# Attention and MLP in one kernel: zeros for 22 early matmuls written first, weight decoding begun later, one sink product for two heads

## The chip, the cores and the metric

The kernel runs on one core of a Trainium2 chip. The time is the device time of one execution in microseconds, the median of three runs. The engines are TensorE (PE, with its weight loads PEld), VectorE (DVE), ScalarE (ACT), GpSimd (POOL) and SyncE (SP), which issues most DMAs.

## The reference

Attention over 4 batches and 8 heads (768 positions, head size 64) with a window of 128 and 4 sink positions, then an MLP on the 3072 tokens:

```python
scores = scale * np.matmul(q, k.transpose(0, 1, 3, 2))
keep = (pos[None, :] < n_sink) | ((rel >= 0) & (rel < window))      # 4, 128
scores = np.where(keep, scores, -1000000000.0)
a = np.exp(scores - max); a = a / (sum + 1e-09)
x = np.matmul(a, v)                       # then heads side by side: 3072 x 512
h = x @ w_in                              # 512 x 2048
g = np.maximum(0.01 * h, h)
return (g @ w_out).astype(np.float32)     # 2048 x 512
```

The MLP's weights arrive as 64-bit floats.

## The kernel before, in words

The queries are cut into 8 units (`NU`): a batch and one half of its positions, 384 queries (`TU`). Units 0 and 1 (`EARLY = 2`) take a short way through attention in plain 32-bit floats; the later ones split their numbers into a high and a low part. Within a unit the 8 heads come one by one, and two heads make a pair (`NPAIR` = 4), which gives one 128-row slice of the MLP's input.

A head has three blocks of queries, j = 0 to 2. For each, `scores` (L264) multiplies queries and keys on PE, `softmax_early` takes the masked maximum on VectorE (L276, `pe`) and the exponential on ScalarE (L278). `normalise_early` (L281 to L288) divides by the sums; `tail_early` transposes on PE (L336, L337, L340) and copies to `pt` on ScalarE (L338, L341). The four sink positions go by their own way: `sk` on GpSimd (L344), one transpose for both heads (L370), and `sn` on VectorE (L374), whose rows hold head and position, with zeros where a row does not belong to a query block. `values` (L406) multiplies with the values of each head, the window blocks first, then the sinks: the left operand is that head's 64 columns of `sv` (from the load `vsraw`), the right one is `sn`, and the product goes into that head's 64 rows of the pair's accumulator `acc` (tile `v`). The rows of `vsraw` are zero in the columns of the other head. After the second head, `emit_x` makes the two parts `xh` (ScalarE, L474) and `xl` (VectorE, L475).

The MLP has 16 steps for each unit: `h` (L519), `g` (L526, L527), its parts `gh` and `gl`, and the sum over steps `o` (L540). A weight pair for one step (`wi`, `wo`) is loaded as raw 64-bit words (`wiraw`, `woraw`, 512 KB each) and decoded by `load_weights`: three operations on VectorE for each of the two (L170, L172, L174, tiles `di`/`do` and `wif`/`wof`), a copy on ScalarE (L178) and a subtraction on GpSimd (L179). In unit 0's MLP step fc the pairs up to fc + 2 are decoded (`AHEAD`). A load beyond the first four waits for the fourth decoding before it (`DEPTH`).

PE's instructions stand in the order in which the code writes them (`MANUAL`): first a loop over the steps of attention until unit 0 is through and a little of unit 1, then MLP steps with attention steps between. The other engines' order, and that of the DMAs, is made by a scheduler. In the first loop `PRE`, `PRE0` and `PRED` say how many weight pairs are decoded there, from which step, and how many steps apart. `WARM` matmuls of zeros (`wz`, L564, tile `warm`), whose product nobody reads, are written before everything else on PE in the code.

```python
        if done >= PRE0 and len(wts) < 2 * min(PRE, (done - PRE0 + 1) // PRED):
            load_weights(len(wts) // 2)
```

`check_weights` later loads raw weights once more (`ciraw`) and looks at their range; it is off the way of the results.

Of the kernel before, what the change touches and what calls it, by code (L numbers as in the profile page):

```python
# [20 lines left out]
P = 128  # L21
# [9 lines left out]
TU = T * P  # L31
# [19 lines left out]
XLP = 3  # L51
VSW = 1
AHEAD = 2
PRE = 3
WARM = 16
DEPTH = 4
PRE0 = 4
PRED = 6
W_LO = 1.125 * 2.0 ** -15
W_HI = 1.875 * 2.0 ** 16  # L60
KSL = ((0, P), (0, W3), (WM, W3)), ((0, W3), (WM, W3), (2 * WM, W3))
# [47 lines left out]


@with_exitstack
def fast_path(ctx, tc, cpool, qk, vu, vs, w_in, w_out, out, ident, lim, masks, tri, diag, negm, wmin, wmax):
    nc = tc.nc
    wpool = ctx.enter_context(tc.tile_pool(name="wpool", bufs=1))
    apool = ctx.enter_context(tc.tile_pool(name="apool", bufs=2))
# [6 lines left out]
    ps_t = ctx.enter_context(tc.tile_pool(name="ps_t", bufs=1, space=PSUM))  # L122
    ps_v = ctx.enter_context(tc.tile_pool(name="ps_v", bufs=1, space=PSUM))

    wz = wpool.tile([P, TU], mybir.dt.bfloat16, name="wz")
    nc.vector.memset(wz, 0.0)
    zeros = iopool.tile([SKR, TU], F32, tag="io", name="zeros")
    nc.vector.memset(zeros, 0.0)
    sts = []
    for half in range(2):  # L130
        st = wpool.tile([SKR, (T - 1 + half) * P], F32R, name=f"st{half}")
# [26 lines left out]
    def load_weights(fc):  # L158
        for nm in ("i", "o"):
            raw = wpool.tile([P, 512, 2], I32, tag=f"w{nm}{fc}", name=f"w{nm}raw{fc}")  # L160
            dma = fetch(raw, nm, fc)
            if len(decoded) >= DEPTH:
                tc.add_manual_dep(dma.ins, decoded[-DEPTH].ins.name,
                                  mybir.DependencyInfo(mybir.DependencyClass.Sync, mybir.DependencyReason.SCHED_ONLY),
                                  reason="pace")
            top, low = raw[:, :, 1], raw[:, :, 0]
            word = ps_t.tile([P, 512], I32, tag="d", name=f"d{nm}{fc}")
            w = iopool.tile([P, 512], F32, tag="io", name=f"w{nm}f{fc}")
            with tc.issue_after(anchor[0].ins):
                nc.vector.tensor_scalar(out=word, in0=top, scalar1=3, scalar2=0x3FFFFFFF,  # L170
                                        op0=ALU.logical_shift_left, op1=ALU.bitwise_and)
            nc.vector.scalar_tensor_tensor(out=word, in0=top, scalar=-0x40000000, in1=word,  # L172
                                           op0=ALU.bitwise_and, op1=ALU.bitwise_or)
            decoded.append(nc.vector.scalar_tensor_tensor(out=w.bitcast(I32), in0=low, scalar=29, in1=word,  # L174
                                                          op0=ALU.logical_shift_right, op1=ALU.bitwise_or))
            both = wpool.tile([P, 2, 512], F32R, tag=f"w{nm}{fc}", name=f"w{nm}{fc}")
            hi, lo = both[:, 0, :], both[:, 1, :]
            nc.scalar.copy(out=hi, in_=w)  # L178
            nc.gpsimd.tensor_tensor(out=lo, in0=w, in1=hi.bitcast(F32), op=ALU.subtract)  # L179
            wts[nm, fc] = (hi, lo)  # L180
# [130 lines left out]
    def segments(half):  # L311
        if half:
            return (0, 0, P), (P, 0, 2 * P), (3 * P, P, 2 * P), (5 * P, 2 * P, P)
        return (0, 0, 2 * P), (2 * P, P, 2 * P), (4 * P, 2 * P, P)
# [70 lines left out]
    def values(u, h, pt, st, state):  # L385
        half = u % 2
        pair, odd = divmod(h, 2)
        q0 = 0 if half else P
        hp = slice(odd * D, (odd + 1) * D)
        lp = slice((1 - odd) * D, (2 - odd) * D)  # L390
        vv, sv = state["v"]
        if u < EARLY:
            if not odd:
                state["acc"] = ps_v.tile([P, 512], F32, tag="v", name=f"v{u}_{h}")
            out = state["acc"][hp, :]
            mms = [(vv[:, kb * P + odd * D:kb * P + (odd + 1) * D], pt[:, 0, po:po + m], qo, m)
                   for kb, (po, qo, m) in enumerate(segments(half))]
            mms.append((sv[0:st.shape[0], hp], st, q0, TU - q0))
        else:
            out = ps_v.tile([P, 512], F32, tag="v", name=f"v{u}_{h}")  # L400
            cs = slice(odd * P, (odd + 1) * P)
            mms = [(vv[:, kb, cs], pt[:, c, po:po + m], qo, m)
                   for kb, (po, qo, m) in enumerate(segments(half)) for c in range(2)]
            mms.append((sv[:, 0, cs], st, q0, TU - q0))
        for c, (l, r, o, m) in enumerate(mms):
            nc.tensor.matmul(out[:, o:o + m], lhsT=l, rhs=r, start=c == 0, stop=c == len(mms) - 1,  # L406
                             skip_group_check=True)
        if u < EARLY:
            x = state["acc"][:, 0:TU]
        else:  # L410
            if not odd:
                state["xf"] = xpool.tile([P, TU], F32, tag="xf", name=f"xf{u}_{pair}")
            x = state["xf"]
            nc.scalar.copy(out=x[hp, :], in_=out[lp, 0:TU])
            nc.vector.tensor_tensor(out=x[hp, :], in0=out[hp, 0:TU], in1=x[hp, :], op=ALU.add)  # L415
        if odd:
            emit_x(u, pair, x)
# [42 lines left out]
    def attend(u, h, pend, state):  # L460
        yield from (attend_early if u < EARLY else attend_late)(u, h, pend, state)
        if h % 2:
            state = state[h // 2 % 2]

            def gather():
                state["st"] = sinks(u, h // 2, state["sk"])
            pend.append((0, gather))
            for o in range(2):
                pend.append((1, lambda o=o: values(u, h - 1 + o, state["pt", o], state["st"], state)))

    def emit_x(u, pair, x):
        xh = xpool.tile([P, TU], F32R, tag=f"xh{pair}", name=f"xh{u}_{pair}")
        xl = xpool.tile([P, TU], F32R, tag=f"xl{pair}", name=f"xl{u}_{pair}")
        nc.scalar.copy(out=xh, in_=x)  # L474
        (nc.gpsimd if EARLY <= u < XLP else nc.vector).tensor_tensor(out=xl, in0=x, in1=xh.bitcast(F32), op=ALU.subtract)  # L475
        xs[u].append((xh, xl))
# [85 lines left out]
    flags = []  # L562
    for _ in range(WARM):
        nc.tensor.matmul(warm[:, 0:TU], lhsT=wz[:, 0:P], rhs=wz, start=True, stop=True)  # L564
# [3 lines left out]
    while done < att_steps + LEAD0:  # L568
        done += 1
        next(stream)  # L570
        if done >= PRE0 and len(wts) < 2 * min(PRE, (done - PRE0 + 1) // PRED):
            load_weights(len(wts) // 2)
# [148 lines left out]
def body(tc, qk0, qk1, vu0, vu1, vs, qT, kT, v, lims, w_in, w_out, out):  # L721
    nc = tc.nc
    w_in = w_in.bitcast(I32)
    w_out = w_out.bitcast(I32)
    with tc.tile_pool(name="cpool", bufs=1) as cpool:
        ident = cpool.tile([P, P], F32, name="ident")
        make_identity(nc, ident)
        negm = cpool.tile([P, 2 * B * H * T], F32, name="negm")
        wmin = cpool.tile([P, 2 * NFC], F32, name="wmin")
        wmax = cpool.tile([P, 2 * NFC], F32, name="wmax")  # L730
        with tc.tile_pool(name="tpool", bufs=1) as tpool:
            lim, masks, tri, diag = build_masks(nc, cpool, tpool, lims)
        flag = fast_path(tc, cpool, (qk0, qk1), (vu0, vu1), vs, w_in, w_out, out, ident, lim, masks, tri, diag,
                  negm, wmin, wmax)
        bad = nc.values_load(flag[0:1, 0:1], min_val=0, max_val=1)
        with tc.If(bad > 0):
            general_path(tc, qT, kT, v, w_in, w_out, out, ident, lim)
# [42 lines left out]
```

## Time and profile before

| what | value |
|---|---|
| median of 3 runs | 749.14 us (748.79 to 749.92) |
| the profiled execution | 746.63 us |
| its span on the core | 745.1 us |
| PE busy | 714.3 us, 96% of the span |
| VectorE, ScalarE, GpSimd busy | 74%, 56%, 50% of the span |
| mean granted clock of PE | 0.992 |
| DMA moved | 77.77 MB, 104 GB/s in the mean |

The profile gives each engine's busy time, the clock granted to PE (1 is full speed), and for idle time what ended it. Rows of the timeline read: start in us, duration in us, engine, line, operation, output from input, how many; in brackets the idle time ahead of it and what ended it. A row may stand for several instructions that follow each other; its duration goes from the first's start to the last's end. Durations of matmuls overlap, since PE pipelines them: what one costs in a full stream is the distance from its start to the next start.

### The profile page before, as it was taken

What the parts mean: (1) busy time and instruction counts of PE and PEld (TensorE: products, weight loads), DVE (VectorE), ACT (ScalarE), POOL (GpSimd) and SP (SyncE); (2) the same over time, 40 slices, a digit from 0 to 9 for tenths busy, and PEclk for the clock granted to TensorE, in tenths of its full rate; (3) what the DMA queues carried; (4) which work ended last, traced back from release to release, by engine and by line L of the source; (5) the groups of instructions that cost most, each with busy time, mean ns of one, the idle gap of its engine ahead of it and who ended that gap; (6) DMA issues with size and microseconds to landing.
All of it is one profiled execution on the core that took longest, in us unless ns stands there. A gap on an engine that the chain in (4) does not pass through costs nothing.

```text
span 745.1 us, 12489 instructions
## 1 busy us (share of the span) xinstructions
PE 714.3 (96%) x3881; PEld 620.6 (83%) x3881; DVE 549.3 (74%) x1749; ACT 420.6 (56%) x1178; POOL 370.0 (50%) x500
## 2 busy tenths in 40 slices
PE   4788999899999999999999999999999999999996
PEld 3446777679999988999988888999889899989995
DVE  6856798847667888888888888889888978733222
ACT  3556567656665666666666666666666655522221
POOL 2303446745445677665666587665666555300000
PEclk9899999999999999999999999999999999999999
DMA  8744675413212343225333443334332321001001
GB/s 295 228 132 127 195 219 172 146 36 99 58 51 65 119 125 114 92 94 156 115 106 102 132 130 100 104 98 153 109 109 78 112 68 40 0 1 43 1 1 48
DMA packets 43755, 77.77 MB, mean 104 GB/s; under 512 B 3616, under 2 KB 26400, under 8 KB 43680
## 3 DMA queue, kind: packets, MB, share of 16 engines
q1 hardware_dynamic: 41520, 74.66, 32.1%
q10 hardware_dynamic: 2160, 2.23, 1.2%
q8 instruction: 33, 0.54, 0.3%
q14 instruction: 42, 0.34, 0.2%
HBM read 70.58 MB, written 6.29 MB: 103 GB/s over the span
## 4 chain that ended last, share of the span: by engine, by line
PE 84%; DVE 9%; ACT 3%; issue 1%; DMA 1%; ACTq 0%; SPq 0%; DVEq 0%
PE o L540 32%; PE h L519 31%; PE v L406 10%; PE s L264 7%; PE t L349 2%; DVE gl L529 2%; DVE zeroi L192 1%; PE t L336 1%; DMA qkn<-in_qk 1%; DVE g L527 1%; DVE pe L276 0%; DVE xf L415 0%; DVE pk L309 0%; PE t L370 0%; PE t L337 0%
## 5 line engine op out<-in xcount | busy, mean ns | idle before, releaser
L519 PE MATMUL h<-xh,wi 128*128 128x384 f32 x1024 | 314.9, 354 | 1.6 <-DVE g L527 1.6
L540 PE MATMUL o<-wo,gh 128*128 128x512 f32 x768 | 244.4, 399 | 0.0
L519 PEld LDWEIGHTS h<-xh,wi 128*128 128x128 f32 x1024 | 190.0, 188 | 16.6 <-issue 2.9
L519 PE MATMUL h<-xl,wi 128*128 128x384 f32 x512 | 172.5, 337 | 0.0
L540 PE MATMUL o<-wo,gl 128*128 128x512 f32 x384 | 151.5, 394 | 0.0
L540 PEld LDWEIGHTS o<-wo,gh 128*128 128x128 f32 x768 | 133.7, 188 | 18.2 <-issue 2.4
L318 POOL TENSOR_SCALAR_AFFINE_SELECT pt<-stg 128x256 fp32r<-128x256 f32 x240 | 101.3, 447 | 83.4 <-DVE stg L357 70.1
L527 DVE TENSOR_TENSOR g<-h,g 128x384 f32<-128x384 f32 x128 | 71.0, 555 | 62.2 <-ACT g L526 60.4
L529 DVE TENSOR_TENSOR gl<-g,gh 128x384 fp32r<-128x384 f32 x112 | 93.3, 833 | 16.5 <-ACT gh L528 15.0
L526 ACT ACTIVATE g<-h 128x384 f32<-128x384 f32 x128 | 62.2, 486 | 71.5 <-PE h L519 71.1
L519 PEld LDWEIGHTS h<-xl,wi 128*128 128x128 f32 x512 | 96.9, 189 | 3.6 <-DVE xl L475 0.2
L230 POOL TENSOR_TENSOR qksp<-qkraw,qksp 64x392 fp32r<-64x392 f32 (+1 forms) x48 | 58.4, 1218 | 64.2 <-issue 47.5
L540 PEld LDWEIGHTS o<-wo,gl 128*128 128x128 f32 x384 | 72.2, 188 | 16.7 <-DVE gl L529 0.3
L303 ACT ACTIVATE pk<-pk,negm 128x128 f32<-128x128 f32 (+1 forms) x144 | 58.1, 403 | 48.6 <-DVE negm L300 47.8
L528 ACT CAST gh<-g 128x384 fp32r<-128x384 f32 x128 | 65.7, 513 | 33.7 <-DVE g L527 31.3
L264 PEld LDWEIGHTS s<-qksp 128*128 128x128 f32 x288 | 53.3, 188 | 5.9
L264 PE MATMUL s<-qksp 128*128 128x260 f32 (+1 forms) x288 | 56.2, 277 | 0.0
L232 POOL TENSOR_TENSOR qksp<-qkraw,qksp 128x384 fp32r<-128x384 f32 x48 | 53.5, 1115 | 3.6
L356 ACT CAST stg<-t 128x128 fp32r<-128x128 f32 x120 | 30.8, 256 | 42.6 <-PE t L349 32.2
L406 PEld LDWEIGHTS v<-pt,vsp 128*128 128x128 f32 x336 | 45.1, 189 | 5.8 <-issue 3.3
L229 ACT CAST qksp<-qkraw 128x776 fp32r<-128x776 f32 (+1 forms) x48 | 42.8, 892 | 11.3 <-PE s L264 11.0
L309 DVE TENSOR_SCALAR pk<-pk,sm 128x132 f32<-128x132 f32 (+1 forms) x120 | 46.0, 383 | 2.4
(131 smaller groups left out, 1088.0 us busy)
## 6 DMA issues: line engine op xcount, KB each, us to landing
qkraw<-in_qk SPq DMA_DIRECT2D x27, 454.0 KB, 3.3
qkraw<-in_qk SPq DMA_DIRECT2D x26, 388.0 KB, 3.1
wiraw<-in_w_in SPq DMA_DIRECT2D x16, 512.0 KB, 3.9
woraw<-in_w_out SPq DMA_DIRECT2D x16, 512.0 KB, 4.0
ciraw<-in_w_in SPq DMA_DIRECT2D x16, 512.0 KB, 3.8
coraw<-in_w_out SPq DMA_DIRECT2D x16, 512.0 KB, 3.6
out<-ob SPq DMA_DIRECT2D x23, 256.0 KB, 2.0
vraw<-in_vu SPq DMA_DIRECT2D x12, 256.0 KB, 2.7
```

The source lines that it names most:

```text
L230: nc.gpsimd.tensor_tensor(out=sp[D:P, TU:TU + n], in0=raw[D:P, TU:TU + n], in1=sp[D:P, TU:TU + n].bitcast(F32), op=ALU.subtract)
L232: nc.gpsimd.tensor_tensor(out=sp[:, TU + n:2 * TU + n], in0=raw[:, 0:TU], in1=sp[:, 0:TU].bitcast(F32), op=ALU.subtract)
L264: nc.tensor.matmul(ps[:, 0:kn], lhsT=sp[:, off + j * P:off + (j + 1) * P], rhs=sp[:, TU + k0:TU + k0 + kn], start=c == 0, stop=c == len(pa ...
L303: nc.scalar.activation(out=w, in_=w, func=AF.Exp, scale=-1.0, bias=neg, accum_out=sm)
L318: nc.gpsimd.affine_select(out=out, in_=src, pattern=([[0, x]] if x > 1 else []) + [[sign, P]], base=-1 if prev else 0, channel_multiplier= ...
L406: nc.tensor.matmul(out[:, o:o + m], lhsT=l, rhs=r, start=c == 0, stop=c == len(mms) - 1, skip_group_check=True)
L519: nc.tensor.matmul(ph[:, 0:TU], lhsT=w[:, cs], rhs=x, start=cc == 0 and c == 0, stop=cc == NCC - 1 and c == 2)
L526: nc.scalar.mul(g, ph[:, 0:TU], 0.01)
L527: anchor[0] = nc.vector.tensor_tensor(out=g, in0=ph[:, 0:TU], in1=g, op=ALU.max)
L528: nc.scalar.copy(out=gh, in_=g)
L529: (nc.gpsimd if u == 0 else nc.vector).tensor_tensor(out=gl, in0=g, in1=gh.bitcast(F32), op=ALU.subtract)
L540: nc.tensor.matmul(po[t], lhsT=gg[:, tsl], rhs=w, start=f == 0 and c == 0, stop=f == NFC - 1 and c == 2)
```

## The change

Four edits. The zeros `wz` are written as VectorE's first instruction, in `body`, and their number of matmuls goes from 16 to 22. Two weight pairs (before: three) are decoded in the first loop, from step 24 on and 12 steps apart (before: step 4 and 6 apart). In units 0 and 1 the sinks of a pair are one product with all 128 columns of `sv` into all 128 rows of `acc`, after the second head's window blocks; before, each head had its own.

```diff
-PRE = 3
-WARM = 16
+PRE = 2
+WARM = 22
 DEPTH = 4
-PRE0 = 4
-PRED = 6
+PRE0 = 24
+PRED = 12
...
-    wz = wpool.tile([P, TU], mybir.dt.bfloat16, name="wz")
-    nc.vector.memset(wz, 0.0)
...
-            mms.append((sv[0:st.shape[0], hp], st, q0, TU - q0))
...
         if u < EARLY:
+            if odd:
+                nc.tensor.matmul(state["acc"][:, q0:TU], lhsT=sv[0:st.shape[0], :], rhs=st, start=False, stop=True,
+                                 skip_group_check=True)
             x = state["acc"][:, 0:TU]
...
     with tc.tile_pool(name="cpool", bufs=1) as cpool:
+        wz = cpool.tile([P, TU], mybir.dt.bfloat16, name="wz")
+        nc.vector.memset(wz, 0.0)
```

What that does to the order of instructions, at three places. In the names, `s_1_0` is the score block 0 of head 1, `qkn_3` or `qkraw_2` the queries and keys of head 3 or 2, `pe_5` the weights of head 5; a number at the end only tells buffers apart. In the changed kernel lines between 126 and 395 are two lower than before.

PE, the start of the program, before (the warm matmuls' rows are cut to the first):

```order
L776 UNCONDITIONAL_BRANCH
L264 MATMUL s_0_0_196<-qkn_0_178 128x128
L264 MATMUL s_0_1_200<-qkn_0_178 128x260
L264 MATMUL s_0_2_204<-qkn_0_178 128x260
L564 LDWEIGHTS wz
L564 MATMUL warm<-wz 128x384
...
L264 MATMUL s_1_0_218<-qkn_1_184 128x128
```

And after:

```order
L778 UNCONDITIONAL_BRANCH
L564 LDWEIGHTS wz
L564 MATMUL warm<-wz 128x384
...
L262 MATMUL s_0_0_202<-qkn_0_184 128x128
L262 MATMUL s_0_1_206<-qkn_0_184 128x260
L262 MATMUL s_0_2_210<-qkn_0_184 128x260
L262 MATMUL s_1_0_224<-qkn_1_190 128x128
```

The warm matmuls moved from between head 0's and head 1's scores to the front of all.

SP, the loads after those of the first three heads, before:

```order
L202 DMA qkraw_2_187<-in_qk 128x776
L153 DMA wiraw_247<-in_w_in 128x4x256
L154 DMA woraw_257<-in_w_out 128x1024
L153 DMA wiraw_306<-in_w_in 128x4x256
L154 DMA woraw_316<-in_w_out 128x1024
L153 DMA ciraw_3055<-in_w_in 128x4x256
L202 DMA qkn_3_213<-in_qk 128x776
L202 DMA qkn_4_268<-in_qk 128x776
L153 DMA wiraw_359<-in_w_in 128x4x256
L202 DMA qkraw_5_330<-in_qk 128x776
```

And after:

```order
L200 DMA qkraw_2_193<-in_qk 128x776
L151 DMA ciraw_3053<-in_w_in 128x4x256
L151 DMA wiraw_410<-in_w_in 128x4x256
L152 DMA woraw_420<-in_w_out 128x1024
L151 DMA wiraw_503<-in_w_in 128x4x256
L152 DMA woraw_513<-in_w_out 128x1024
L200 DMA qkn_3_219<-in_qk 128x776
L200 DMA qkn_4_254<-in_qk 128x776
L200 DMA qkraw_5_296<-in_qk 128x776
L200 DMA qkn_6_343<-in_qk 128x776
```

Head 3's load stays behind the same five weight loads, of which the check copy is now the first; the third pair's load left its place among the heads' loads.

VectorE, heads 1 and 2, before (the read-outs `negm` behind each L276 are left out here and below):

```order
L170 TENSOR_SCALAR di_249<-wiraw_247 128x512
L276 ISA pe_2_274,negm<-s_2_0_277,m_84 128x128
...
L276 ISA pe_2_274,negm<-s_2_1_281,wide_143 128x260
...
L172 SCALAR_TENSOR_TENSOR di_249<-wiraw_247,di_249 128x512
L281 TENSOR_SCALAR sm_1_216<-sm_1_216 128x3
L174 SCALAR_TENSOR_TENSOR wif_250<-wiraw_247,di_249 128x512
L282 RECIPROCAL sm_1_216<-sm_1_216 128x3
L170 TENSOR_SCALAR do_259<-woraw_257 128x512
L288 TENSOR_SCALAR pe_1_215<-pe_1_215,sm_1_216 128x128
```

After, the first decoding stands between heads 5 and 6:

```order
L274 ISA pe_5_387,negm<-s_5_1_398,wide_143 128x260
...
L168 TENSOR_SCALAR di_412<-wiraw_410 128x512
L274 ISA pe_5_387,negm<-s_5_2_433,wide_151 128x260
...
L170 SCALAR_TENSOR_TENSOR di_412<-wiraw_410,di_412 128x512
L475 TENSOR_TENSOR xl_1_407<-v_2_394,xh_1_406 128x384
L172 SCALAR_TENSOR_TENSOR wif_413<-wiraw_410,di_412 128x512
L274 ISA pe_6_458,negm<-s_6_0_461,m_86 128x128
...
L168 TENSOR_SCALAR do_422<-woraw_420 128x512
```

The decoding moved from heads 1 to 4 to heads 5 to 7; its last operation of the two pairs stands just ahead of `xl_2`, and the third pair's six stand around `xl_3` and the MLP's first `g`.

More of the change, by code (lines that the diff above doesn't have):

```diff
@@ L111, in fast_path @@
 @with_exitstack
-def fast_path(ctx, tc, cpool, qk, vu, vs, w_in, w_out, out, ident, lim, masks, tri, diag, negm, wmin, wmax):
+def fast_path(ctx, tc, cpool, qk, vu, vs, w_in, w_out, out, ident, wz, lim, masks, tri, diag, negm, wmin, wmax):
     nc = tc.nc
@@ L732, in body @@
             lim, masks, tri, diag = build_masks(nc, cpool, tpool, lims)
-        flag = fast_path(tc, cpool, (qk0, qk1), (vu0, vu1), vs, w_in, w_out, out, ident, lim, masks, tri, diag,
+        flag = fast_path(tc, cpool, (qk0, qk1), (vu0, vu1), vs, w_in, w_out, out, ident, wz, lim, masks, tri, diag,
                   negm, wmin, wmax)
```

## Prediction

> **What bounds the kernel now.** I read the page first (busy shares, slices), then stages by window, then the timeline of the first 70 us, the DMA landings and the PE's waits.
>
> ```profile
> span 745.1 us, 12489 instructions
> PE 714.3 (96%) x3881; PEld 620.6 (83%) x3881; DVE 549.3 (74%) x1749; ACT 420.6 (56%) x1178; POOL 370.0 (50%) x500
> PE   4788999899999999999999999999999999999996
> PEclk9899999999999999999999999999999999999999
> 0.00:20.00 20.00, 10.00 (x45) 6.92 (x46) 14.16 (x57) 7.57 (x24) 5.50 (x19) 0.89 0.82 283
> 20.00:40.00 20.00, 16.16 (x66) 9.23 (x64) 15.76 (x48) 9.21 (x30) 6.95 (x8) 0.85 0.67 207
> 40.00:60.00 20.00, 17.23 (x83) 10.18 (x82) 10.11 (x45) 11.96 (x44) 0.76 (x4) 1.00 0.44 127
> 150.00:200.00 50.00, 50.00 (x276) 43.19 (x275) 29.54 (x107) 29.70 (x87) 24.14 (x34) 1.00 0.21 62
> ```
>
> The columns of a window are its length, then busy us (and instructions) of PE, PEld, DVE, ACT, POOL, the granted clock, the DMA share and GB/s. From 60 us on TensorE (PE) is full: 50.00 of 50.00 us in the last window. Of the 30.8 us in which it idles (745.1 less 714.3), 16.6 lie before 60 us (60 less 10.00, 16.16 and 17.23), and in the first two windows its clock is also below 1. PE runs its instructions in the written order, so the change can gain in two ways: PE reaches the first product of the MLP (58.74 us) sooner, or has less to do after it.
>
> **The change part by part. Warm-up and the first heads.**
>
> ```profile
> 0.94 0.38 DVE L104 MEMSET diag<- 24x384 f32 x1 [0.94 <-PEq L770]
> 6.12 2.53 PE L264 MATMUL s<-qkn 128*128 128x128 f32 x6 [6.12 <-DMA qkn<-in_qk]
> 8.00 0.28 DVE L276 CUSTOM_DVE_ANT_0 pe<-s,m 128x128 f32<-128x128 f32 x1
> 8.44 3.02 PE L564 MATMUL warm<-wz 128*128 128x384 bf16 x16
> 8.72 0.49 ACT L278 ACTIVATE pe<-pe,negm 128x260 f32<-128x260 f32 x1
> 10.31 0.82 DVE L288 TENSOR_SCALAR pe<-pe,sm 128x128 f32<-128x128 f32 x3
> 11.30 0.82 PE L264 MATMUL s<-qkn 128*128 128x128 f32 x4
> 9.58 3.67 SPq L202 DMA_DIRECT2D qkn<-in_qk  x2
> qkn<-in_qk SPq DMA_DIRECT2D x1, 388.0 KB, 8.2
> 20.14 0.63 PE L264 MATMUL s<-qkn 128*128 128x128 f32 x2
> 8.00:9.00 1.00, 1.00 (x4) 0.45 (x3) 0.84 (x6) 0.68 (x3) 0.75 (x5) 1.00 0.82 170
> 9.00:10.00 1.00, 1.00 (x8) 0.59 (x7) 0.33 (x3) 0.87 (x4) 0.00 (x0) 1.00 1.10 387
> ```
>
> Now the 16 warm matmuls stand behind head 0's scores and hold head 1's from 8.44 to 11.30: 2.86 us. With the zeros written at about 1.1 us (VectorE's first instruction starts at 0.94), the 22 can start at about 1.3. At the pace of these 16 (0.179 us) they take 3.9 us and end at 5.2, before head 0's data land at 6.12; at half that pace they end at 9.2. Either way VectorE's first softmax is held by the masks until about 8, so head 0 moves by -0.2 to +1.6 us and head 1's scores come 1 to 3 us sooner. The six more warm matmuls cost nothing: that wait for data covers them; without the cover they are 1.1 us.
>
> That is not passed on whole. On SP's queue head 3's load stands behind five weight loads of 512 KB, before and after. Before, it was issued at 9.58 and took 8.2 us: landed at 17.8. After, one of the five (the check copy) is put first and can go out at about 5 us, which fills the dip of 8 to 9 us (170 GB/s, beside 387 in the next microsecond): 217 GB/s for 1 us are 0.22 MB, 0.6 us at 387. Bounds: 0 (the dip stays) to 1 us (all of it). I take 0.5: landing at 17.3. PE is there earlier: head 0 is normalised near 11.1 as before (10.31 + 0.82); head 1's third scores and softmax wait for its transposes and end near 12.1; the exponential and its sum (0.49 + 0.2), the sums' reciprocal (0.35), the normalisation (0.82) and the sink copy and transposes (0.6) make about 14.6. So head 3's scores start at 17.3 instead of 20.14, and 2.7 us of wait on DMA is new. It also absorbs the worst case of the warm-up above.
>
> ```profile
> 15.00:16.00 1.00, 0.00 (x0) 0.00 (x0) 1.00 (x5) 0.31 (x3) 0.00 (x0) 0.89 1.11 425
> 16.00:17.00 1.00, 0.09 (x1) 0.12 (x1) 1.00 (x3) 0.50 (x1) 0.42 (x1) 0.50 1.03 406
> 22.00:23.00 1.00, 1.00 (x5) 0.59 (x4) 1.00 (x3) 0.33 (x1) 0.00 (x0) 0.70 0.96 328
> 20.70 2.21 PE L406 MATMUL v<-pt,vraw 128*64 128x256 f32 x6
> 43.98 1.30 PE L406 MATMUL v<-pt,vraw 128*64 128x256 f32 x6
> 25.85 0.33 PE L340 MATMUL t<-ident,pe 128*128 128x128 f32 x1
> 39.20 0.33 PE L340 MATMUL t<-ident,pe 128*128 128x128 f32 x1
> 48.21 0.33 PE L340 MATMUL t<-ident,pe 128*128 128x128 f32 x1
> 22.85 0.64 PE L406 MATMUL v<-sn,vsraw 16*64 16x256 f32 x2
> 23.42 0.71 PE L264 MATMUL s<-qkn 128*128 128x260 f32 x2
> ```
>
> The clock: PE idle from 13.85 brought the grant to 0.50 near 15.9, and it came back near 22.7, 4.5 us after PE had work again. Six value products take 2.21 us in it and 1.30 at full clock. After the change PE is sparse from 8.7 to 17.3 (some 2.7 us of work), so I expect half clock at 17.3, back within 2.4 to 5.8 us. Head 3's first scores, a set of value products, the second scores, another set and one sink product are 0.3 + 1.2 + 0.6 + 1.2 + 0.6 = 4.0 us at full clock (row starts). At 1.30/2.21 = 0.59 of it for 4.1 us, the middle, 2.4 are done, and 1.6 are left: 5.7 (5.0 to 6.4 at the ends). So head 2's first transpose (25.85 before) comes at 23.0: 2.85 us sooner; at full clock it would be 4.5.
>
> The Trainium skill, TensorE: Matmul & The Clock Gate, section "Part 1: The HAM clock gate", says that warmth is about 3.4 us of sustained activity, however many matmuls, and that an idle window of that length throttles again. By that rule the 22 early matmuls buy nothing at 17 us, as the term of 2.85 has it; if warmth lasted, the term would be 4.5. [...]
>
> **Heads 2 and 3 lose their decoding.** From head 2's first transpose to head 4's took 13.35 us (25.85 to 39.20) with decoding between, and the same stretch one pair later 9.01 without (39.20 to 48.21). After the change the earlier one is like the later one, less one sink product, 0.57 (22.85 to 23.42): 8.44. Lead at head 4's transpose: 2.85 + 13.35 - 8.44 = 7.8 (7 to 9.5).
>
> **Heads 4 to 7 gain it.**
>
> ```profile
> 13.28 0.69 DVE L170 TENSOR_SCALAR di<-wiraw 128x512 int32<-128x512 int32 x1
> 40.00 0.43 DVE L276 CUSTOM_DVE_ANT_0 pe<-s,wide 128x260 f32<-128x260 f32 x1 [2.06 <-PE s L264]
> 40.20:49.20 9.00, 7.97 (x39) 4.71 (x39) 5.26 (x25) 4.94 (x20) 0.38 (x2) 1.00 0.47 128
> 16.48 1.81 DVE L288 TENSOR_SCALAR pe<-pe,sm 128x128 f32<-128x128 f32 x3
> 16.58 1.30 POOL L179 TENSOR_TENSOR wi<-wif,wi 128x512 fp32r<-128x512 f32 x1 [5.20 <-ACT wi L178]
> ```
>
> Two pairs are 12 VectorE operations of 0.69: 8.3 us, and by the order all stand between head 5's second softmax and pair 2's split (`xl_2`). Cover: one fits the 2.06 us of idle before 40.00 (0.69), and VectorE idles 3.74 of the 9.00 us behind it (9.00 less 5.26). Left are 8.3 - 4.4 = 3.9; the bounds are 0 (all absorbed, were the idle longer) and 8.3 (none). Overlapped issue saves about 0.08 each, so I take 3.6. GpSimd's subtraction beside a normalisation stretches that from 0.82 to 1.81 us; one half overlap of the four: 0.4. While VectorE does this, PE waits; like the idle from 13.85 that can cost the clock, and I take an even chance of one more cold spell, 4.1 x 0.41 = 1.65: 0.8. What waits behind each decode operation is the next softmax, then the transposes, then PE. Against it pair 3's sink product goes, 0.57; that of pair 2 lies in PE's wait and is counted at nothing. Lead at the first MLP product (58.74): 7.8 - 3.6 - 0.4 - 0.8 + 0.6 = 3.6 (1 to 7).
>
> **Third pair and the second unit's sinks.**
>
> ```profile
> 60.23 0.56 DVE L475 TENSOR_TENSOR xl<-v,xh 128x384 fp32r<-128x384 f32 x1 [2.74 <-ACT xh L474]
> 62.89 0.55 DVE L527 TENSOR_TENSOR g<-h,g 128x384 f32<-128x384 f32 x1
> 63.49 0.44 PE L519 MATMUL h<-xh,wi 128*128 128x384 f32 x1 [1.59 <-DVE g L527]
> 80.02 0.85 PE L406 MATMUL v<-sn,vsraw 24*64 24x384 f32 x2
> 80.80 0.74 PE L540 MATMUL o<-wo,gh 128*128 128x512 f32 x2
> ```
>
> The third pair's six operations, 4.1 us, now come with the MLP's start. Two fit the 2.74 us of idle before `xl_3`, the rest pushes the second normalisation back by about 0.8 us, hardly the first `g`. I put 0.5 us of new PE wait (bounds -0.3, since one operation leaves the place ahead of `g`, and 2.7, the four that are not covered). In the second unit PE is full, so each removed sink product counts whole: 0.78 (80.02 to 80.80), four of them 3.1.
>
> Sum: 3.6 + 3.1 - 0.5 = 6.2 us. The profiled execution took 746.63 us (span 745.1), the median of the runs is 749.14, 2.5 more; the saving is the same against either: 740.4 in such a profile, 742.9 in the median.
>
> **Rivals.**
> - The clock stays full at 17 us and in the later gaps. For it: some work falls in every few us. Against: 0.50 after a like gap. Gain 6.2 + 1.65 + 0.8 = 8.7: 740.4.
> - Slower: VectorE sets the pace from head 4 into the MLP. If none of the moved decoding is covered (8.3, and 4.1 for the third pair) and every overlap with GpSimd costs 1 us (four: 4.0), the 7.8 + 0.6 + 3.1 = 11.5 turn into 4.9 us lost: 754.0. It decides from 11.5 exposed us on. For it: 13.35 against 9.01 us. Against: VectorE idles 3.74 of 9.00 us there.
> - The DMA order hurts: the check copy, put first, delays heads 1 and 2 by its transfer (512 KB, about 1.35 us at 388 GB/s), the dip is not filled (0.5), and the third pair stalls PE by 2.7 (2.2 more). Gain 6.2 - 4.0 = 2.2: 746.9.
> - The merged sink does not do what it says: with twice the columns of weights it costs twice, and 0.57 + 3.1 in the sum (and 0.57 each in pairs 0 and 1) goes. Gain 6.2 - 4.8 = 1.4: 747.7. Against: its moving operand is as long as that of one of the two.
>
> **How the numbers follow.** Less than 0.2% (1.5 us) can't be told from no change here. Chances: the sum as worked out 0.62, full clock 0.15, DMA order 0.12, sinks 0.05, VectorE 0.06. The first two are faster; of the DMA case two thirds, and of the sink case a part. Faster 0.86, same 0.08, slower 0.06. The range reaches from 739.8 (the full-clock case and 0.6 for its own terms) to 747.0 (the DMA case); VectorE's and most of the sink case are left out. The sum's own bounds on the lead, 1 to 7, stand for 745.5 to 739.5.
>
> **What would show it.** Warm matmuls first on PE, ended before 9 us; head 3's scores released by the DMA near 17.3; granted clock 0.50 there until 20 to 23; head 4's first transpose near 31.4; decoding packed into the next 13 us and PE waiting for it; the first MLP product near 55; sink products one per pair, 0.78 us in the second unit; PE as full after 60 us as before. It is wrong if head 3's load lands much later or earlier, or if PE's wait at the start of the MLP (1.59 us now) grows by more than 2 us.

## The result and the profile after

| | before | after |
|---|---|---|
| median of the runs on the same chip | 748.97 us (748.79 to 749.92) | 739.47 us (738.49 to 740.68) |
| ratio | | 0.9873, 95% interval 0.9859 to 0.9887 |
| profiled execution, span | 746.63, 745.1 us | 739.14, 737.7 us |
| first product of the MLP on PE | 58.74 us | 52.59 us |
| from there to the end | 686.4 us | 685.1 us |

The changed kernel is 9.5 us faster (8.5 to 10.6 by the interval). The forecast was 6.2 us and 742.9 us, with a range from 739.8 to 747.0: the time lies 0.3 us below the range. In the two profiles the saving is 7.5 us, of which 6.15 come ahead of the MLP's first product and 1.3 behind it.

The page of the profile after: span, engines, PE's slices; then windows of it (length; busy us and count of PE, PEld, DVE, ACT, POOL; granted clock; DMA share; GB/s).

```profile
span 737.7 us, 12461 instructions
PE 712.0 (97%) x3871; PEld 621.5 (84%) x3871; DVE 546.9 (74%) x1749; ACT 421.4 (57%) x1178; POOL 370.4 (50%) x500
PE   7788999899999999999999999999999999999995
0.00:20.00 20.00, 15.18 (x64) 9.15 (x65) 11.90 (x62) 8.47 (x27) 4.75 (x19) 0.91 0.78 277
20.00:40.00 20.00, 15.79 (x74) 9.97 (x72) 13.93 (x52) 11.66 (x40) 3.11 (x5) 0.91 0.49 153
40.00:60.00 20.00, 16.01 (x75) 10.52 (x75) 15.95 (x45) 12.87 (x38) 6.38 (x8) 1.00 0.60 201
140.00:145.00 5.00, 4.60 (x16) 3.62 (x17) 0.97 (x3) 1.42 (x4) 2.25 (x2) 0.66 0.00 0
```

PE is 5.2 us busier in the first window: 2.2 are zeros (5.23 us in place of 3.02), which now fill time in which it waited for data, and 3.0 are work that comes sooner, since head 3's scores start at 17.09 in place of 20.14. VectorE has moved as the change says: 13.93 instead of 15.76 us in the second window, 15.95 instead of 10.11 in the third. The last row is new: a spell of half clock (a stretch in which the granted clock is 0.50) in 140 to 145 us, where the profile before has 1.00.

The timeline of after, PE's rows and one of VectorE (start, duration, engine, line, operation; in brackets the idle time ahead and what ended it):

```profile
1.19 5.23 PE L564 MATMUL warm<-wz 128*128 128x384 bf16 x22 [1.19 <-DVE wz L727]
6.25 1.33 PE L262 MATMUL s<-qkn 128*128 128x128 f32 x6
17.09 0.49 PE L262 MATMUL s<-qkn 128*128 128x128 f32 x2
20.59 0.69 PE L407 MATMUL v<-sn,vsraw 16*128 16x256 f32 x2
21.22 0.33 PE L338 MATMUL t<-ident,pe 128*128 128x128 f32 x1
29.82 0.33 PE L338 MATMUL t<-ident,pe 128*128 128x128 f32 x1
34.97 0.45 PE L338 MATMUL t<-ident,pe 128*128 128x128 f32 x1 [2.10 <-DVE pe L286]
45.01 1.60 DVE L286 TENSOR_SCALAR pe<-pe,sm 128x128 f32<-128x128 f32 x3
52.59 0.44 PE L519 MATMUL h<-xh,wi 128*128 128x384 f32 x1
56.62 0.44 PE L519 MATMUL h<-xh,wi 128*128 128x384 f32 x1 [1.00 <-DVE g L527]
60.38 0.33 PE L334 MATMUL t<-ident,pe 128*128 128x128 f32 x1 [1.17 <-ACT pt L336]
```

These are, in order: the zeros; head 0's scores; head 3's scores; the merged sink product; the first transposes of heads 2, 4 and 5; a normalisation stretched beside GpSimd; the MLP's first product, and PE's two longest waits in the 8 us behind it. Head 2's transpose comes 4.6 us sooner than before, head 4's 9.4, the MLP 6.15.

### The profile page after: what moved, and what is told of

It is laid out like the page before. It is cut to its first block, busy times and chain, and to the rows that moved or that the text cites. A ratio compares the mean times of both kernels' runs of the same rounds, so it can differ in the third digit from the quotient of the medians.

```text
span 737.7 us, 12461 instructions
## 1 busy us (share of the span) xinstructions
PE 712.0 (97%) x3871; PEld 621.5 (84%) x3871; DVE 546.9 (74%) x1749; ACT 421.4 (57%) x1178; POOL 370.4 (50%) x500
## 4 chain that ended last, share of the span: by engine, by line
PE 83%; DVE 9%; ACT 3%; issue 2%; DMA 1%; POOL 0%; ACTq 0%; POOLq 0%; DVEq 0%
PE o L540 33%; PE h L519 32%; PE v L403 8%; PE s L262 6%; PE t L347 2%; DVE gl L529 2%; DVE zeroi L190 1%; PE v L407 1%; DMA woraw<-in_w_out 1%; PE t L334 1%; DVE g L527 1%; DVE pe L274 1%; DVE xf L415 0%; DVE pk L307 0%; ACT pe L276 0%
```

## The experiments

Ratios are to the kernel before, run on the same chip. Savings in microseconds are one less the ratio, times the median of before there.

**The kernel before once more, and each edit alone.** No edit in the first; the zeros moved and raised to 22 in the second, the table of the decoding in the third, the merged product in the fourth.

```diff
# warm_only
-WARM = 16
+WARM = 22
...
-    wz = wpool.tile([P, TU], mybir.dt.bfloat16, name="wz")
-    nc.vector.memset(wz, 0.0)
...
+        wz = cpool.tile([P, TU], mybir.dt.bfloat16, name="wz")
+        nc.vector.memset(wz, 0.0)
         ident = cpool.tile([P, P], F32, name="ident")
# decode_only
-PRE = 3
+PRE = 2
...
-PRE0 = 4
+PRE0 = 24
-PRED = 6
+PRED = 12
# sink_only
-            mms.append((sv[0:st.shape[0], hp], st, q0, TU - q0))
...
+            if odd:
+                nc.tensor.matmul(state["acc"][:, q0:TU], lhsT=sv[0:st.shape[0], :], rhs=st, start=False, stop=True,
+                                 skip_group_check=True)
```

> The kernel before, unchanged, profiled once more and timed beside itself. Theory A (the profile of before that I worked from was a lucky draw of the clock, 2.5 us under the median): time within 0.1% of the other runs of before, near 749, mean granted clock near 0.988 in most runs, and where a run is faster its clock is higher by about 0.0014 for each us; the profile shows a half-clock spell that the first one lacked. Rival B (the 2.5 us is something else, such as the profiler's): clock the same in fast and slow runs, and the new profile again near 746.6 us.

> Only the zeros first and 22 warm matmuls ahead of head 0; decoding and sinks as before. Theory A (each part earns by itself): head 1's scores near 8 us instead of 11.3, but decoding keeps VectorE full from 13 us on, so 1.5 to 2.5 us faster, about 747. Rival B (the warm-up is worth nothing where decoding sets the pace): within 0.7 us of before. Rival C (it earns its whole 2.86 us of blocked PE and more by a warm clock): 4 us or more faster.

> Only the decoding: two pairs in the first loop, from step 24, 12 steps apart; 16 warm matmuls behind head 0's scores and a sink product for each head, as before. Theory A: heads 1 to 4 free of decoding gain some 7, heads 5 to 7 give back some 4, third pair 0.5: 3 us faster, about 746. Rival B (the place of the decoding is nothing by itself, since VectorE's work is the same): within 1 us. Rival C (it is nearly all of the gain): 6 us or more.

> Only the merged sink product in the first two units. Theory A: 3.1 us in the second unit where PE is full, and 0.57 for each of two to four pairs in the first: 3.5 to 5 us faster, about 745. Rival B (VectorE holds the section before 150 us, and PE's shorter work there turns into wait): about 2 us. Rival C (the merged product costs twice): no change.

| kernel | median us (runs) | ratio, 95% interval | saving us |
|---|---|---|---|
| before again | 749.78 (12) | 1.0005 [0.9996, 1.0014] | -0.4 |
| zeros alone | 745.29 (6) | 0.9954 [0.9938, 0.9970] | 3.4 |
| decoding alone | 746.18 (9) | 0.9973 [0.9960, 0.9987] | 2.0 |
| sinks alone | 744.45 (6) | 0.9949 [0.9932, 0.9965] | 3.8 |

The three savings add to 9.2 us, against 9.5 together. None of the edits is idle, and none needs another to work: each interval lies below 1. The zeros are worth more than theory A's 1.5 to 2.5 us and less than rival C's 4 (interval 2.2 to 4.6), the decoding less than theory A's 3 (1.0 to 3.0), and the sinks lie in theory A's bounds.

The profile of the unchanged kernel (749.78 us, span 748.4) is the more telling one: it is the same program as in the prediction's rows, and it starts the MLP 3.8 us later.

```profile
20.00:40.00 20.00, 16.16 (x54) 9.35 (x52) 16.29 (x48) 9.67 (x30) 6.80 (x8) 0.69 0.64 201
8.38 4.56 PE L564 MATMUL warm<-wz 128*128 128x384 bf16 x16
21.63 0.64 PE L264 MATMUL s<-qkn 128*128 128x128 f32 x2
22.20 2.40 PE L406 MATMUL v<-pt,vraw 128*64 128x256 f32 x6
26.73 2.40 PE L406 MATMUL v<-pt,vraw 128*64 128x256 f32 x6
29.63 0.33 PE L340 MATMUL t<-ident,pe 128*128 128x128 f32 x1
43.01 0.33 PE L340 MATMUL t<-ident,pe 128*128 128x128 f32 x1
62.55 0.45 PE L519 MATMUL h<-xh,wi 128*128 128x384 f32 x1
```

The 16 zeros take 4.56 us instead of 3.02, and both sets of value products run at half clock (2.40 us each), where in the other execution only the first did (2.21). From head 3's scores to head 2's transpose are 8.0 us instead of 5.7. Head 2's transpose comes at 29.63 instead of 25.85, 3.8 us later (1.5 by the slower zeros, 2.3 behind head 3's scores), and nothing from there to the MLP differs: 13.38 us to head 4's transpose (13.35), 19.54 on to the MLP (19.54).

The time and the longer half clock (18.9 to 29.1 us, in the first profile 15.9 to 22.7) are as theory A has it; the link between time and mean clock that it names is not there. Of the 75 timed executions of before in these experiments, 46 have a mean clock of 0.989, and they take from 746.7 to 750.6 us. The clock column is blind to part of this: it reads 1.00 in the first microseconds also where PE is slow (head 0's six score matmuls take 2.53 us at 6.12 in before and 1.33 at 6.25 in after, both at 1.00). So that the usual execution is slow in the way of this profile is likely, not shown. The fastest of the 75 took 746.73 us; the profile of 746.63 lies below them all.

The profile of sink_only:

```profile
58.29 0.45 PE L521 MATMUL h<-xh,wi 128*128 128x384 f32 x1
83.98 0.91 PE L409 MATMUL v<-sn,vsraw 24*128 24x384 f32 x2
84.81 0.45 PE L521 MATMUL h<-xh,wi 128*128 128x384 f32 x1
```

From the MLP's start to the end it takes 682.9 us; in before_again this takes 685.9, 3.0 us more. The rows give the same: a merged product costs 0.83 us from start to start (83.98 to 84.81), where each of the two had cost 0.78; that is 0.73 less for a pair and 2.9 for four. The 0.8 that are left of the saving of 3.8 would lie before the MLP, and are no more than the intervals leave open.

**The changed kernel once more, and zeros put into the gaps.** The kernels' own work is not touched: 12 more matmuls of zeros ahead of the first transposes of heads 1 and 3 (before), or 8, 4 and 9 ahead of those of heads 0, 1 and 5 (after).

```diff
     def tail_early(u, h, j, w, pt, sk):
         half = u % 2
+        n = {1: 12, 3: 12}.get(h, 0) if u == 0 and j == 0 else 0      # after: {0: 8, 1: 4, 5: 9}
+        if n:
+            idle = ps_h.tile([P, 512], F32, tag="h", name=f"idle{h}")
+        for _ in range(n):
+            nc.tensor.matmul(idle[:, 0:TU], lhsT=wz[:, 0:P], rhs=wz, start=True, stop=True)
```

> The changed kernel once more, beside the three that follow. Both theories: 739 to 740 us, with runs 2 to 3 us apart; its first MLP product between 50 and 56 us by where the cold spells fall.

> The kernel before with 12 more matmuls of zeros at each of two places where PE waits for VectorE in the first unit: ahead of the first transposes of heads 1 and 3; nothing else is changed. Theory A (the clock is what the idle costs): granted clock 1 from 9 us to 60, no spell of half clock there, the first MLP product near 55 and 2.5 to 4 us faster, near 745.5. Rival B (the path there is VectorE's, so a cold PE costs nothing): same time within 0.7 us, or slower by what the added matmuls hold up.

> The changed kernel with 8, 4 and 9 more matmuls of zeros ahead of the first transposes of heads 0, 1 and 5, where PE waits for VectorE. Theory A (cold spells near 11 and 35 us remain after the change and cost time): both are gone, 1 to 2.5 us faster than the changed kernel, 737 to 738.5. Head 3's load then sets the start of its scores near 17, as forecast. Rival B (VectorE is the path): within 0.7 us of the changed kernel.

After again: 739.27 us, ratio 0.9863 [0.9844, 0.9882]. Its profile (739.98 us, span 738.3):

```profile
16.45 0.80 PE L262 MATMUL s<-qkn 128*128 128x128 f32 x2 [0.81 <-DMA qkn<-in_qk]
17.18 2.40 PE L403 MATMUL v<-pt,vraw 128*64 128x256 f32 x6
22.03 0.33 PE L338 MATMUL t<-ident,pe 128*128 128x128 f32 x1
30.64 0.33 PE L338 MATMUL t<-ident,pe 128*128 128x128 f32 x1
40.00:60.00 20.00, 17.09 (x66) 10.15 (x64) 13.08 (x39) 10.60 (x32) 3.39 (x6) 0.83 0.50 160
55.95 0.44 PE L519 MATMUL h<-xh,wi 128*128 128x384 f32 x1
140.00:145.00 5.00, 3.11 (x18) 2.65 (x17) 3.79 (x12) 3.74 (x10) 4.32 (x5) 1.00 0.01 4
```

Heads 2 and 4 come 0.8 us later than in the first profile of after, the MLP 3.4 later (half clock in 47 to 54 us), and yet the execution is only 0.8 us longer, because it has no half clock at 140 to 145: from the MLP's first product to the end it takes 682.35 us instead of 685.1. The spell costs 5 x 0.34 = 1.7 us of that by its clock, and PE's own end moves by 1.9 (from the MLP's first to the last matmul 677.15 and 675.27 us); the other 0.9 lie in the stretch behind PE's last matmul. Both profiles have a wait of 1.9 us for VectorE just there (the profile names the decoding operation `wof`); in one the clock falls behind it, in the other it does not. Twelve of the fourteen profiles on record have that wait (1.9 to 2.0 us), the kernel before among them, and in three the clock falls to half behind it: after, after_fill and after_no_zeros (there in 145 to 150 us).

The profile of before_fill has a clock of 1.00 in every window up to the last matmuls:

```profile
20.00:40.00 20.00, 16.31 (x81) 9.37 (x80) 17.34 (x54) 11.00 (x38) 6.07 (x8) 1.00 0.68 203
14.25 2.11 PE L337 MATMUL idle<-wz 128*128 128x384 bf16 x12
58.00 0.45 PE L524 MATMUL h<-xh,wi 128*128 128x384 f32 x1
```

That execution took 745.21 us, the fastest of its 12; the median is 749.32, ratio 1.0005 [0.9993, 1.0016]: no gain, as rival B has it. Even so the MLP starts at 58.00, not at theory A's 55, and only 0.7 us sooner than in the first profile of before. The mean clocks of its executions are 0.990 to 0.998, those of before beside it 0.986 to 0.990, and the time is the same; what the added zeros cost elsewhere, if that is the reason, its one profile does not show. After_fill has 738.61, ratio 0.9851 [0.9830, 0.9871], not to be told from after: rival B. Its profile has a clock of 1.00 up to 40 us, so the two spells that were aimed at are gone, but there is another behind them, beside the one at 140 (0.66):

```profile
40.00:60.00 20.00, 15.17 (x68) 9.99 (x67) 14.96 (x40) 13.60 (x39) 6.77 (x8) 0.91 0.61 197
```

Filling gaps with zeros does not pay here.

**The zeros taken away.** In the changed kernel and in the kernel before, without any other edit.

```diff
-WARM = 22                       # after_no_zeros
+WARM = 0
-WARM = 16                       # before_no_zeros
+WARM = 0
```

> The changed kernel with no warm matmul at all. Theory A (their gain is that they no longer stand between heads 0 and 1; warmth at 7 us is lost by 11): head 0's scores cold from 6.1 to 8.7, head 1's behind them, within 1 us of the changed kernel. Rival B (the early warmth carries through): 2.5 us or more slower.

> The kernel before without its 16 matmuls of zeros (they stood behind head 0's scores and ahead of head 1's, waited for DVE, and held the array up for 2.86 us in one profile and longer in the other). Theory A, what the zeros cost in before is their place: without them head 1's scores start 2 to 3 us earlier, head 2's transpose comes some 2 us earlier, and the time falls by 1 to 3 us: 746 to 748 us. Rival B, what the zeros bring is warmth, and their place costs little: without them the clock is halved through heads 0 to 3, and the time rises by 1 to 3 us: 750 to 752. If it comes out within 0.8 us of before, place and warmth weigh the same in before, and the 3.4 us that the zeros alone earned when they were moved to the front are the two together.

Without the zeros the changed kernel takes 741.94 us, 0.9904 [0.9887, 0.9922], 2.7 us more than with them (medians on one chip): rival B, the early warmth carries through. Its profile (742.78 us) shows how far:

```profile
6.22 3.82 PE L262 MATMUL s<-qkn 128*128 128x128 f32 x10 [6.22 <-DMA qkn<-in_qk]
16.65 1.07 PE L262 MATMUL s<-qkraw 128*128 128x260 f32 x2
18.15 0.63 PE L262 MATMUL s<-qkn 128*128 128x128 f32 x2
22.52 0.33 PE L338 MATMUL t<-ident,pe 128*128 128x128 f32 x1
56.01 0.44 PE L519 MATMUL h<-xh,wi 128*128 128x384 f32 x1
```

Two score matmuls still take 1.07 us at 16.65, where they take 0.60 at 16.08 in after. Head 3's scores start at 18.15 (17.09 and 16.45 in the two profiles with zeros), head 2's transpose at 22.52 (21.22 and 22.03), the MLP at 56.01 (52.59 and 55.95).

The kernel before takes 746.39 us (12 runs), 0.9965 [0.9952, 0.9978], 2.6 us less than with them: theory A of that run. So where they stood the zeros cost more than they brought. Of the 3.4 us that moving them earns, 2.6 are had by taking them away, and 0.8 come from their new place; the intervals leave it open whether that is less than the 2.7 in the changed kernel.

The profiled execution of before without zeros took 746.67 us, close to that kernel's median, and reaches the MLP at nearly the same time as the profile on which the prediction was built (58.74):

```profile
20.00:40.00 20.00, 15.55 (x61) 8.85 (x59) 16.44 (x46) 8.62 (x27) 6.93 (x8) 0.78 0.62 201
24.81 0.33 PE L340 MATMUL t<-ident,pe 128*128 128x128 f32 x1
58.66 0.44 PE L519 MATMUL h<-xh,wi 128*128 128x384 f32 x1
```

Read with the two medians, that profile of before was an execution in which the 16 zeros cost next to nothing; in the median they cost 2.6 us. The second is measured; the reading of the single execution rests on one profile of each kernel.

**The wait at 140 us, and the change without its decoding.** Both edits are to the changed kernel: eight matmuls of zeros put just ahead of the wait at 140 us, and the decoding's table as it was before the change.

```diff
# after_late_fill
     def tail_early(u, h, j, w, pt, sk):
         half = u % 2
+        if (u, h, j) == (1, 7, 2):
+            idle = ps_t.tile([P, 512], F32, tag="t", name="idle")
+            for _ in range(8):
+                nc.tensor.matmul(idle[:, 0:TU], lhsT=wz[:, 0:P], rhs=wz, start=True, stop=True)
# warm_and_sink
-PRE = 2
+PRE = 3
...
-PRE0 = 24
+PRE0 = 4
-PRED = 12
+PRED = 6
```

> The changed kernel with 8 more matmuls of zeros just ahead of the transposes for which TensorE waited 1.9 us (138.5 to 140.4 in its profile), in its place behind the products of the MLP. Theory A, the half clock from 140.8 to 144.0 came of that wait and takes about 2.8 us back in many of the executions: no half clock at 140 to 145, 682.4 us from the MLP's first product to the end, and a median of 737.5 to 738.5. Rival B, the spell is rare, or the wait only moves: the median stays at 739 to 740, and what the profile shows at 140 is no part of the measured saving.

> The zeros at the front and the merged sinks, without the early decoding. Theory A, the parts are worth the same alone and together: 3.4 + 3.8 = 7.2 us below before, a median near 741.5, and about 2 us above the changed kernel. Rival B, the decoding ahead uses time that only the warm start lays free, and is worth more in company (the forecast had it shorten the interval of heads 2 and 3 by 5.1 us and cost 4.2 us later): 742.5 to 744.

```profile
138.39 1.47 PE L334 MATMUL idle<-wz 128*128 128x384 bf16 x8
140.57 0.33 PE L338 MATMUL t<-ident,pe 128*128 128x128 f32 x1 [0.71 <-DVE wof L172]
140.00:145.00 5.00, 4.43 (x23) 3.52 (x24) 1.74 (x6) 2.59 (x6) 2.27 (x3) 1.00 0.00 0
```

With the eight matmuls the wait is 0.71 us and the clock stays at 1.00 in this profile (737.8 us). The median is 737.97, inside theory A's bounds, but the six executions reach from 736.38 to 744.28 and the interval, 0.9845 to 0.9910, holds the changed kernel's ratio. From the MLP's first product to the end it takes 683.9 us, not 682.4. That the wait brings the spell fits this profile, but nine others have the wait and no spell; that its removal shortens the kernel is not shown.

Without the decoding ahead: 742.53 us, 0.9918 [0.9894, 0.9942], that is 6.1 us (4.3 to 7.9) below before. Theory A said 7.2, rival B 5.1 to 6.6; the interval takes in both, so whether the decoding is worth more in company than its 2.0 alone is open.

**Both fills together**, the 8, 4, 9 of after_fill and the 8 of after_late_fill.

```diff
+        n = {(0, 0, 0): 8, (0, 1, 0): 4, (0, 5, 0): 9, (1, 7, 2): 8}.get((u, h, j), 0)
...
```

> The changed kernel with both sets of added zero matmuls: 8, 4 and 9 ahead of the first transposes of heads 0, 1 and 5 of the first unit, and 8 ahead of the transposes of the second unit for which TensorE waited from 138.5 to 140.4 us. Alone they gave medians of 738.61 and 737.97, against 739.27 to 739.47 without, neither told apart from it. Theory A, each takes away a half-clock spell that the changed kernel has in many executions, and the two add up: a median of 736.5 to 737.5, and an interval that lies below the changed kernel's 0.9863 to 0.9873. Rival B, the spells come from where the clock's windows fall, and the added work only shifts them: 738 to 739.5.

738.43 us (737.85 to 739.16), 0.9870 [0.9851, 0.9890]: rival B. Its profile has 1.00 in 140 to 145 us and, like that of after_fill, 0.91 from 40 to 60. No version tried here is shown to beat the changed kernel.

## Why the prediction was right and wrong

**The step that failed** is the last sentence of the sum: "the saving is the same against either: 740.4 in such a profile, 742.9 in the median." In such a profile it was right within 1.3 us: the two profiled executions of the changed kernel took 739.14 and 739.98. But the median of its runs is 739.47, 0.3 above its first profile, not 2.5. The 2.5 us between the profile of before and the median were taken for an offset that stays. The runs show them to be, in the main, part of what the change removes: without its zeros the kernel before has a median of 746.39, 2.6 less, and its profile stands there too (746.67). Before_again shows one way in which they arise: an execution at 749.78 whose MLP starts 3.8 us later, all of it ahead of head 2's transpose, by slower zeros and a longer half clock behind them. Of the 3.4 us between forecast and median some 2.2 are this (2.5 less 0.3), the other 1.2 the terms below. The range had the same fault, and was drawn narrower than the sum's own bounds: a lead of 7 us stood for 739.5.

That 740.4 came so close is in part luck. Against the profile of before, the first profile of after leads by 6.15 us at the MLP's start where 3.6 were forecast, and gains 1.3 behind it where 2.6 were; in the second it is 2.8 and 4.0. The errors have opposite signs.

**Warm-up.** The zeros run from 1.19 to 6.42 us, released by VectorE, and end before 9 us as said; 5.23 us lies between the 3.9 and 7.9 of the two paces. In this profile head 0's scores start at 6.25 instead of 6.12. In after_again the zeros take 6.08 us and the scores start at 7.10, but head 0's first transpose waits for VectorE in both (10.88 and 10.97), so "the six more warm matmuls cost nothing" holds there too. Head 1's scores start at 7.94 instead of 11.30, 3.4 us sooner, a little beyond the forecast's 1 to 3. That the early matmuls "buy nothing at 17 us" holds in the second profile alone, and they are worth something in both on the way there: without them PE is slow from its first score to 16.65 and beyond, head 3's scores start 1.1 to 1.7 us later, and the median is 2.7 us longer.

**Head 3's scores.** Forecast 17.3, a wait of 2.7 us on DMA. They start at 17.09 in one profile and at 16.45 in the other, and the load of their weights into PE is released by the DMA in both. PE's own wait is small, 0.03 and 0.81 us, because the heads before came 1.0 to 2.5 us later than forecast (the sink transpose, their last instruction, starts at 15.37 or 16.79 and takes 0.27; forecast 14.6); in the first profile heads 0 to 2 ran at half clock between 11 and 14 us. The landing was forecast 0.2 to 0.9 us too late. Neither miss costs much, since the later of the two decides. Head 4's transpose comes at 29.82 and 30.64 in the two profiles of after, at 39.20 and 43.01 in those of before.

**The clock at 17 us.** Forecast half clock until 20 to 23, head 2's transpose at 23.0. In one profile the clock is full there (value products 1.30 us, transpose at 21.22: the rival's course at this place), in the other it is 0.50 until 19 to 20 (first set 2.40 us, transpose at 22.03). The forecast was 1.0 to 1.8 us late. In the profile that it was built on, the grant fell at 15.9 us, 2.0 us after PE ran idle at 13.85, which is sooner than by the 3.4 us of idle that the prediction argued with. The Trainium skill, TensorE: Matmul & The Clock Gate, section "Part 1: The HAM clock gate", says that the window is free-running, so that the count of slow matmuls differs from run to run, and advises not to fit to it. The traces agree: the same program has half clock from 15.9 to 22.7 us in one profile of before and from 18.9 to 29.1 in the other. The Trainium skill, same page and section, also puts the ramp below 1% of a kernel's span; here two executions of one program differ by 3.8 of 748 us at the MLP's start, 0.5%, which is as much as the terms that were to be forecast.

**Heads 2 and 3.** Forecast 8.44 us from head 2's to head 4's transpose, measured 8.60 and 8.61.

**Heads 4 to 7.** Forecast a net cost of 4.2 us (lead from 7.8 to 3.6). In the profiles after and before the lead goes from 9.4 to 6.15: 3.2. PE waits 2.10 us for the normalisation at 34.97, half clock follows it, and the 1.60 us normalisation beside GpSimd is there, all as written. In after_again a second spell (47 to 54 us) brings the cost to 5.8 and the MLP's start to 55.95, the forecast's 55; the even chance of one more spell was a fair price for something that comes or does not.

**Third pair and sinks.** Of the 0.5 us for the third pair, 0.2 are seen in after: PE's wait for `g` falls from 1.59 to 1.00 us, and that for ScalarE's copy `pt` grows from 0.34 to 1.17. In decode_only the rest takes 685.8 us, as in before_again (685.9). The sinks are right: 3.1 forecast, 3.0 measured. The merged product costs nearly what one head's product did: from start to start 0.63 us in the first unit (20.59 to 21.22) against 0.57, and 0.83 in the second against 0.78.

**The rivals.** The merged sink does what it says (3.8 us alone, where that rival has no gain from it). VectorE does not set the pace as its rival has it: that needs 11.5 us of exposed work, and the cost from head 4 to the MLP was 3.2 and 5.8. The DMA order did no harm: head 3's load landed at 17.8 in the profile of before, and by 17.09 and 16.45 in those of after. "The clock stays full" gave 740.4 from the same carried-over median. "PE as full after 60 us as before" missed the spell at 140.

## What to carry to other kernels

A profile is one execution. Where it lies 2.5 us off the median and the change is worth 6, first find what the usual execution has that the profiled one has not: a second profile of the same program showed such an execution here, and the difference sat in the very instructions that the change moved and those just behind them. In this kernel warm-up work paid where TensorE had nothing else to do, ahead of the first data (2.7 us); behind the first scores it cost 2.6 us more than it gave. A product whose left operand has unused columns served two heads for little more than the price of one (0.83 us against 0.78), and where TensorE is full the other product is saved almost whole.

## What the runs showed that was not expected

- The same program's first heads take 3.8 us more or less (MLP at 58.74 or 62.55) by the pace of the zeros and by where the half clock falls.
- A wait of 1.9 us in a full stream is followed by half clock in one execution (0.66 in 140 to 145) and not in another (1.00), which cost 1.7 to 1.9 us; of twelve profiles with the wait, three have the spell.
- Between the first recorded change of clock and the last matmuls, the spells of half clock in the fourteen profiles all last 3.4, 6.8 or 10.2 us (140.8 to 144.2 in after, 15.9 to 22.7 in before, 18.9 to 29.1 in before_again).
- Filling gaps with zeros raised the mean clock of before from some 0.989 to some 0.994 and left its median at 749.3. The mean does not count the slow first microseconds, in which the column reads 1.00.
